# Placing a weight's sign on ScalarE, and squaring the first chunk's features on VectorE

## The chip, the cores and the metric

The kernel runs on one core of a Trainium2 chip. The core has a tensor engine (PE, with its weight loads PEld), a vector engine (DVE), a scalar engine (ACT), a general engine (POOL), and SP, whose queue issues transfers. Each engine works through its own list of instructions in order; they wait for each other by semaphores. The metric is device time in microseconds of one execution. The profile is of one execution, and its times are counted from the start of its span.

## What is computed

Attention of 8 batches, 8 heads, 576 positions and 64 dimensions, of which heads 0 to 3 see the last 32 positions and heads 4 to 7 every 32nd position. Its output goes as 4608 tokens of 512 features through an MLP with squared rectification:

```python
def _attn_ref(q, k, v):
    scores = scale * np.matmul(q, k.transpose(0, 1, 3, 2))
    mask_local = (rel >= 0) & (rel < stride)
    mask_strided = (rel >= 0) & (pos[None, :] % stride == pos[:, None] % stride)
    ...
    return np.matmul(attn, v).astype(np.float32)

def _moe_ref(x, w_in, w_out):
    h = np.maximum(x @ w_in, 0.0)
    return (h * h @ w_out).astype(np.float32)
```

`w_in` (512 x 2048) and `w_out` (2048 x 512) arrive as 64-bit floats. The kernel turns each into two 32-bit parts, a high and a low one, and each matrix product of the MLP is made of three: high x high, high x low, low x high.

## The kernel before

The tokens are cut into 12 chunks of 384. Chunk 0's attention comes first (`first` and `late`, 4 pairs of heads). Then a loop of steps `s` runs the MLP: step `s` belongs to chunk `c = s // 16` and to feature tile `j = s % 16` of 128 features. `up(c, j)` makes 12 matmuls into a PSUM tile `ph` (the trace's `h`), rectifies and squares it, copies it to `gh` and puts the remainder into `gl`; `down(c, j)` takes `gh` and `gl` with `w_out` in 9 matmuls into the outputs `y`. `down` runs two steps behind `up`. The attention of later chunks is laid between these steps: `local` and `strided` make chunk 1's while chunk 0's MLP runs.

The weights are converted by `convert` (lines 146 to 180) while attention and chunk 0's MLP run. There are 16 weight tiles `k` of 1024 columns, `w_in` and `w_out` in turn; tiles 0 to 11 come whole, tiles 12 to 15 in two halves each through the pool `s3` of five buffers, which the strided attention uses as well. A 64-bit float is two 32-bit words, `raw[:, :, 0]` and `raw[:, :, 1]`, the second with sign, exponent and upper mantissa. For each tile, `scale(k)` (line 152, ACT) takes that second word as a 32-bit float and multiplies it by 2^-112, which sets the exponent as a 32-bit float needs it three bits further up. Then, for each half of 512 columns, these run one after the other:

- `z` (line 164, ACT): the first word, scaled to its upper three bits, into a PSUM tile;
- the sign merge (line 167, DVE): the sign bit of the second word is put into `z`;
- the shift (line 168, DVE): the second word is shifted left by three, which throws its sign away, and `z` is merged in; this is the weight as a 32-bit float;
- `split`: the high part (line 171, ACT) and the low part (line 172, POOL). It is put on the lists one half later, behind the next half's `z`.

`zbank` names the PSUM banks that `z` may use: two at first, and one (bank 4) from step `s == LATER` (3) on, since the attention of chunk 1 needs the other. The conversion runs two halves a step in chunk 0 (`WRATE`). Its instructions are put behind `gh` of the step (`behind({"a": last["gh"]}, ...)`), and it is the list of ACT that this orders. Six halves are put ahead of the loop. The order of each engine's list is set when the kernel is built, by a planner that goes by its own estimates.

`p_t` are two tiles of 128 x 384 in SBUF, cleared at the start (line 114), of which the attention of chunks 2 and later (`pe_head`) writes parts, and in which it counts on zeros elsewhere. `p_t[1]` also serves as operand of the matmuls that keep PE busy at the start.

Of the kernel before, what the change touches and what calls it, by code (L numbers as in the profile page):

```python
# [11 lines left out]
AF = mybir.ActivationFunctionType  # L12
ALU = mybir.AluOpType
# [13 lines left out]
NFT = DF // P  # L27
# [22 lines left out]
def f32(ap):  # L50
    return ap.bitcast(F32)
# [35 lines left out]
def attn_moe(ctx: ExitStack, tc, qk_l, v_l, qk_d, v_d, qk_p, v_p, f_s, q_s, k_s, v_s, w_in, w_out, masks, eye, out):  # L87
    nc = tc.nc
# [13 lines left out]
    def psum(i, nm):  # L102

        return ps.tile([P, 512], F32, name=nm, tag=f"ps{i}")
# [4 lines left out]
    ident = const.tile([P, P], F32, name="ident")  # L109


    p_t = [const.tile([P, NW, QC], F32, name=f"p_t{i}") for i in range(2)]
    for t in p_t:
        nc.gpsimd.memset(t, 0.0)
# [16 lines left out]
    def fetch(k):  # L131

        p, which = order[k]
        src = (w_out if which else w_in)[p].bitcast(U32).rearrange("p (n t) -> p n t", t=2)
        if k < 12:
            raw = wpool.tile([P, 1024, 2], U32, name=f"raw{k}", tag=f"w{k + 8 if k < 8 else k + 4}")
            nc.sync.dma_start(out=raw, in_=src)
            raws[k] = [(raw, slice(0, 1024))]
        else:
            raws[k] = []  # L140
            for i in range(0, 1024, WP):
                raw = spool.tile([P, WP, 2], U32, name=f"raw{k}_{i}", tag="s3", bufs=5)
                nc.sync.dma_start(out=raw, in_=src[:, i : i + WP])
                raws[k].append((raw, slice(i, i + WP)))

    def convert():

        split = None

        def scale(k):  # L150
            for raw, _ in raws[k]:
                nc.scalar.mul(f32(raw[:, :, 1]), f32(raw[:, :, 1]), 2.0**-112)  # L152

        scale(0)
        for k in range(NFT):
            p, which = order[k]
            t = wpool.tile([P, 2, 1024], F32R, name=f"w{which}_{p}", tag=f"w{k}")
            (wo if which else wi)[p] = t[:, 0], t[:, 1]
            cuts = [(raw[:, i : i + WP], sl.start + i) for raw, sl in raws.pop(k) for i in range(0, sl.stop - sl.start, WP)]
            for raw, at in cuts:  # L160

                z = psum(zbank[next(zturn) % len(zbank)], f"z{k}_{at}").bitcast(U32)
                w, hi, lo = raw[:, :, 1], t[:, 0, at : at + WP], t[:, 1, at : at + WP]
                first_step = nc.scalar.activation(z, raw[:, :, 0], AF.Copy, bias=-0.49, scale=2.0**-29 * (1 - 2.0**-9))  # L164
                if split:
                    split()
                nc.vector.scalar_tensor_tensor(out=z, in0=w, scalar=0x80000000, in1=z, op0=ALU.bitwise_and, op1=ALU.bitwise_or)  # L167
                last["v"] = nc.vector.scalar_tensor_tensor(out=w, in0=w, scalar=3, in1=z, op0=ALU.logical_shift_left, op1=ALU.bitwise_or)  # L168

                def split(w=w, hi=hi, lo=lo, at=at, k=k):  # L170
                    last["a"] = nc.scalar.copy(hi, f32(w))  # L171
                    last["g"] = nc.gpsimd.tensor_sub(lo, f32(w), f32(hi))  # L172
                    if at and 4 <= k < 12:
                        fetch(k + 4)

                if not at and k + 1 < NFT and k + 1 in raws:
                    with tc.issue_after(first_step.ins):
                        scale(k + 1)
                yield
        split()  # L180
# [266 lines left out]
    def up(c, j):  # L447
        x = xt[c]
        p, o = divmod(j, 2)
        ph = psum((c * NFT + j) % 3, f"h{c}_{j}")  # L450
        n = 0
        for kt in range(4):
            kind, kk = "ls"[kt // 2], kt % 2
            xh, xl = x[kind, "h"][:, kk, :], x[kind, "l"][:, kk, :]
            wsl = slice(kt * 256 + o * P, kt * 256 + (o + 1) * P)
            for w, xx in ((wi[p][0], xh), (wi[p][0], xl), (wi[p][1], xh)):
                done = nc.tensor.matmul(ph[:, :TC], w[:, wsl], xx, start=n == 0, stop=n == 11)  # L457
                n += 1
        gh = gpool.tile([P, TC], F32R, name=f"gh{c}_{j}", tag="gh")
        gl = gpool.tile([P, TC], F32R, name=f"gl{c}_{j}", tag="gl")  # L460
        g = ph[:, :TC]
        nc.scalar.activation(g, g, AF.Relu)  # L462
        nc.scalar.activation(g, g, AF.Square)  # L463
        last["gh"] = nc.scalar.copy(gh, g)  # L464
        nc.vector.tensor_sub(gl, g, f32(gh))  # L465
        g_tiles[c, j] = gh, gl
        return done

    def down(c, j):
        gh, gl = g_tiles.pop((c, j))  # L470
        p, o = divmod(j, 2)
        if j == 0:
            y_ps[c] = [ps_y.tile([P, DM], F32, name=f"y{c}_{t}", tag="psy") for t in range(NTT)]
        wsl = slice(o * DM, (o + 1) * DM)
        for t in range(NTT):
            sl = slice(t * P, (t + 1) * P)
            for k, (g, w) in enumerate(((gh, wo[p][0]), (gh, wo[p][1]), (gl, wo[p][0]))):
                done = nc.tensor.matmul(y_ps[c][t], g[:, sl], w[:, wsl], start=j == 0 and k == 0, stop=j == NFT - 1 and k == 2)  # L478
        if j == NFT - 1:
            for t in range(NTT):  # L480
                y = ypool.tile([P, DM], F32, name=f"ysb{c}_{t}", tag="ysb")
                (nc.scalar.copy if t == 1 else nc.vector.tensor_copy)(y, y_ps[c][t])
                nc.sync.dma_start(out=out[c * TC + t * P : c * TC + (t + 1) * P, :], in_=y)
        return done


    def run(gen):
        for _ in gen:
            pass
# [37 lines left out]
    def local(c):  # L527
        heads = [pair_at(c, pr, True, pr, "3") for pr in range(2)]
        for h in (0, 0, 1, 0, 1, 0, 0, 1, 1, 1):
            next(heads[h])  # L530
            yield
# [15 lines left out]
    def take(c, which):  # L547

        if NPLAIN <= c < NCHUNK:
            for h in map(int, which):  # L550
                if (c, h) not in heads:
                    heads[c, h] = pe_head(c, h)
                with ExitStack() as st:
                    for i in (last["pe"], *(weights_end.values() if c == NPLAIN else ())):
                        st.enter_context(tc.issue_after(i.ins))
                    last.pop("mm", None)
                    next(heads[c, h])
                    last["pe"] = last.get("mm", last["pe"])
# [55 lines left out]
    for s in range(NS + 2):  # L614
        c, j = divmod(s, NFT)
        if s < NFT:
            up(c, j)
            if s >= 2:
                last["pe"] = down(*divmod(s - 2, NFT))

        elif s % 2 == 0:
            before, between, rest = plan[j // 2]
            for part, slots, two in (up, (s, s + 1), before), (down, (s - 2, s - 1), between):
                take(c + 1, two)
                with tc.issue_after(last["pe"].ins):
                    for i in slots:
                        if 0 <= i < NS:
                            last["mm"] = part(*divmod(i, NFT))
                last["pe"] = last["mm"]
            take(c + 1, rest)  # L630
        if j == NFT - 2:
            take(c + 2, "010")
        if c == 0:

            weights = behind({"a": last["gh"]}, ungated)
            for _ in range(WRATE):
                if next(weights, "end") != "end":
                    weights_end = {e: last[e] for e in "agsv"}
        if s == LATER:
            zbank = (4,)  # L640
        if c + 1 < NCHUNK and s >= LATER:
            j0 = LATER if c == 0 else 0
            if j == j0:
                lo, st = local(c + 1) if c == 0 else iter(()), strided(c + 1)
                if c == 0:
                    lo, st = behind(heads_end, lo), behind(heads_end, st)
                if c == 1:
                    st = behind(weights_end, st)
                cost = sum(2 * sum(range(i0 + 1, i1 + 1)) + 10 for _, i0, i1, _ in ranges(c + 1))
                dl = ds = 0  # L650
            fl, fs = ((j + 1 - j0) / n for n in SPREAD[min(c, 1)])
            while dl < fl * 10 and next(lo, "end") != "end":
                dl += 1
            while ds < fs * cost:
                k = next(st, "end")
                if k == "end":
                    break
                ds += k
            if j == NFT - 1:
                run(lo)  # L660
                run(st)
# [76 lines left out]
```

## Time and profile before

| | us |
|---|---|
| median of 3 runs | 892.15 (891.91 to 892.57) |
| the profiled execution | 893.0 |
| its span | 891.2 |
| DVE, lines 167 and 168, 32 each | 22.1 and 21.9 |
| ACT, lines 164 and 171, 32 each | 20.6 and 21.0 |
| ACT, line 152, 20 | 19.3 |
| POOL, line 172, 32 | 42.2 |

A row of the profile names the line, the engine, the operation, and `out<-in` by the program's names; then a count, the busy time, the mean of one in ns, and the idle time of the engine just before them with what ended it. `raw`, `z` and `w` belong to the conversion, `h`, `gh`, `gl` and `y` to the MLP; `pq`, `sc`, `pp`, `qkvs` to the strided attention, `e`, `nm`, `rs`, `pt`, `b` to the pairs of heads. In a row of stretches, engines follow in the order PE, PEld, DVE, ACT, POOL.

### The profile page before, as it was taken

What the parts mean: (1) busy time and instruction counts of PE and PEld (TensorE: products, weight loads), DVE (VectorE), ACT (ScalarE), POOL (GpSimd) and SP (SyncE); (2) the same over time, 40 slices, a digit from 0 to 9 for tenths busy, and PEclk for the clock granted to TensorE, in tenths of its full rate; (3) what the DMA queues carried; (4) which work ended last, traced back from release to release, by engine and by line L of the source; (5) the groups of instructions that cost most, each with busy time, mean ns of one, the idle gap of its engine ahead of it and who ended that gap; (6) DMA issues with size and microseconds to landing.
All of it is one profiled execution on the core that took longest, in us unless ns stands there. A gap on an engine that the chain in (4) does not pass through costs nothing.

```text
span 891.2 us, 14804 instructions
## 1 busy us (share of the span) xinstructions
PE 874.0 (98%) x4744; PEld 790.8 (89%) x4744; DVE 652.2 (73%) x1836; ACT 579.8 (65%) x1526; POOL 676.2 (76%) x720
## 2 busy tenths in 40 slices
PE   8898999999999999999999999999999999999997
PEld 7686789999999999899999999998999999998996
DVE  5689778878878878879678778787787887883111
ACT  5897986666757656757747657666665675664332
POOL 4679678788887889989888997997988899782000
PEclk9899999999999999999999999999999999999999
DMA  9833351323113114104202312211031121000000
GB/s 352 351 138 116 106 179 48 106 70 96 60 45 125 42 39 150 43 13 123 67 17 74 102 31 73 76 57 56 30 114 60 31 70 50 18 2 1 36 1 35
DMA packets 26797, 71.40 MB, mean 80 GB/s; under 512 B 2976, under 2 KB 8736, under 8 KB 25184
## 3 DMA queue, kind: packets, MB, share of 16 engines
q1 hardware_dynamic: 26432, 70.14, 23.8%
q8 instruction: 37, 0.61, 0.3%
q14 instruction: 40, 0.33, 0.1%
q10 hardware_dynamic: 288, 0.33, 0.1%
HBM read 61.01 MB, written 9.44 MB: 79 GB/s over the span
## 4 chain that ended last, share of the span: by engine, by line
PE 91%; ACT 4%; DVE 2%; POOL 2%; issue 1%; DVEq 0%; POOLq 0%; ACTq 0%
PE h L457 43%; PE y L478 42%; PE s L233 2%; PE o L279 2%; POOL w L172 1%; ACT e L340 1%; ACT raw L152 1%; DVE raw L168 1%; PE b L316 1%; DVE z L167 1%; PE w_ps L573 1%; ACT z L164 1%; ACT w L171 1%; PE b L373 0%; ACT pt L355 0%
## 5 line engine op out<-in xcount | busy, mean ns | idle before, releaser
L478 PE MATMUL y<-w,gh 128*128 128x512 f32 x1152 | 358.0, 392 | 4.3 <-ACT w L171 2.7
L478 PEld LDWEIGHTS y<-w,gh 128*128 128x128 f32 x1152 | 212.3, 188 | 46.2 <-ACT w L171 3.5
L457 PE MATMUL h<-xlh,w 128*128 128x384 f32 x768 | 229.4, 340 | 1.1 <-POOL w L172 0.6
L457 PE MATMUL h<-xsh,w 128*128 128x384 f32 x768 | 225.6, 335 | 0.8 <-POOL w L172 0.5
L478 PE MATMUL y<-w,gl 128*128 128x512 f32 x576 | 224.5, 392 | 0.7 <-DVE gl L465 0.7
L429 POOL TENSOR_TENSOR pp<-vs,sc 128x448 f32<-128x448 f32 (+10 forms) x192 | 189.7, 1012 | 40.3 <-DVE qs L430 18.1
L407 POOL TENSOR_TENSOR pq<-ks,qs 128x512 f32<-128x512 f32 (+2 forms) x192 | 197.8, 1049 | 18.8 <-DVE sc L408 14.4
L465 DVE TENSOR_TENSOR gl<-h,gh 128x384 fp32r<-128x384 f32 x192 | 105.4, 549 | 83.4 <-ACT gh L464 82.0
L462 ACT ACTIVATE h<-h 128x384 f32<-128x384 f32 x192 | 90.6, 473 | 109.5 <-PE h L457 106.5
L464 ACT CAST gh<-h 128x384 fp32r<-128x384 f32 x192 | 91.4, 477 | 105.6 <-PE y L478 104.6
L408 DVE TENSOR_REDUCE sc<-pq 128x8 f32<-128x512 f32 (+4 forms) x228 | 119.3, 534 | 43.9 <-POOL pq L407 41.8
L457 PEld LDWEIGHTS h<-xlh,w 128*128 128x128 f32 x768 | 141.8, 188 | 4.5 <-POOL w L172 1.3
L457 PEld LDWEIGHTS h<-xsh,w 128*128 128x128 f32 x768 | 141.2, 188 | 2.0 <-POOL w L172 0.9
L430 DVE TENSOR_REDUCE qs<-pp 128x64 f32<-128x448 f32 (+11 forms) x192 | 106.9, 563 | 32.0 <-POOL pp L429 30.4
L457 PE MATMUL h<-xll,w 128*128 128x384 f32 x384 | 129.3, 337 | 0.0
L478 PEld LDWEIGHTS y<-w,gl 128*128 128x128 f32 x576 | 108.0, 188 | 23.8 <-DVE gl L465 1.2
L457 PE MATMUL h<-xsl,w 128*128 128x384 f32 x384 | 128.2, 334 | 0.4 <-DVE xsl L378 0.4
L463 ACT ACTIVATE h<-h 128x384 f32<-128x384 f32 x192 | 90.5, 473 | 3.7
L258 DVE STREAM_TRANSPOSE p_t<-e 32x128 f32<-32x128 f32 x240 | 72.3, 301 | 10.3 <-ACT e L247 6.0
L457 PEld LDWEIGHTS h<-xll,w 128*128 128x128 f32 x384 | 72.5, 189 | 2.1
L457 PEld LDWEIGHTS h<-xsl,w 128*128 128x128 f32 x384 | 72.0, 188 | 0.6 <-DVE xsl L378 0.6
L242 ACT ACTIVATE e<-e,nm 96x128 f32<-96x128 f32 x160 | 62.5, 392 | 9.3 <-DVE nm L225 8.0
(85 smaller groups left out, 1088.5 us busy)
## 6 DMA issues: line engine op xcount, KB each, us to landing
qk<-qk_l SPq DMA_DIRECT2D x24, 400.0 KB, 3.2
y<-ysb SPq DMA_DIRECT2D x36, 256.0 KB, 3.2
raw<-w_in SPq DMA_DIRECT2D x7, 1024.0 KB, 10.8
qk<-qk_l SPq DMA_DIRECT2D x16, 416.0 KB, 3.2
vs<-v_s SPq DMA_DIRECT2D x10, 576.0 KB, 3.7
raw<-w_out SPq DMA_DIRECT2D x5, 1024.0 KB, 12.9
v<-v_l SPq DMA_DIRECT2D x40, 128.0 KB, 2.0
ks<-k_s SPq DMA_DIRECT2D x8, 576.0 KB, 3.8
```

Source lines behind the costliest of these rows:

```text
L242: nc.scalar.activation(e[:QC, cut(w)], e[:QC, cut(w)], AF.Exp, bias=nmax[:QC, w : w + 1], scale=-1.0, accum_out=ssum[:QC, w, :1])
L258: nc.vector.transpose(out=pt[STR * k : STR * (k + 1), :, STR * r : STR * (r + 1)], in_=e.rearrange("p (w k) -> p w k", k=KW)[STR * r : STR ...
L407: nc.gpsimd.tensor_mul(pv, kt[:, a : a + m, :], qt[:, i - i0 : i - i0 + 1, :].broadcast_to([P, m, D]))
L408: nc.vector.tensor_reduce(out=sc[:, i - i0, a : a + m], in_=pv, op=ALU.add, axis=AX.X)
L429: nc.gpsimd.tensor_mul(pv, vt[:, a : a + nd, :n], sc[:, il : il + 1, :n].broadcast_to([P, nd, n]))
L430: nc.vector.tensor_reduce(out=ot[:, il, a : a + nd], in_=pv, op=ALU.add, axis=AX.X)
L457: done = nc.tensor.matmul(ph[:, :TC], w[:, wsl], xx, start=n == 0, stop=n == 11)
L462: nc.scalar.activation(g, g, AF.Relu)
L463: nc.scalar.activation(g, g, AF.Square)
L464: last["gh"] = nc.scalar.copy(gh, g)
L465: nc.vector.tensor_sub(gl, g, f32(gh))
L478: done = nc.tensor.matmul(y_ps[c][t], g[:, sl], w[:, wsl], start=j == 0 and k == 0, stop=j == NFT - 1 and k == 2)
```

## The change

Two parts. In the conversion, the multiplication by 2^-112 becomes a rectification with a slope for negative values of -2^32. A negative word comes out positive and 2^32 times as large, which is one set bit in its exponent; the shift by three moves this bit to where the sign stands. A positive word comes out as before. So the sign merge is dropped.

In chunk 0, the square is no longer made by ACT. ACT writes the rectified features into `p_t` (turn about), and DVE multiplies the features, rectified once more, with them, into PSUM, from where `gh` and `gl` are made as before. Chunks 1 to 11 keep rectification and square on ACT. As `p_t` now gets other contents, it is cleared once more in step 15.

```diff
         def scale(k):
             for raw, _ in raws[k]:
-                nc.scalar.mul(f32(raw[:, :, 1]), f32(raw[:, :, 1]), 2.0**-112)
+                nc.scalar.activation(f32(raw[:, :, 1]), f32(raw[:, :, 1]), AF.Prelu, scale=2.0**-112, alpha=-(2.0**32))
...
                 if split:
                     split()
-                nc.vector.scalar_tensor_tensor(out=z, in0=w, scalar=0x80000000, in1=z, op0=ALU.bitwise_and, op1=ALU.bitwise_or)
                 last["v"] = nc.vector.scalar_tensor_tensor(out=w, in0=w, scalar=3, in1=z, op0=ALU.logical_shift_left, op1=ALU.bitwise_or)
...
         g = ph[:, :TC]
-        nc.scalar.activation(g, g, AF.Relu)
-        nc.scalar.activation(g, g, AF.Square)
+        if c == 0:
+            r = p_t[j % 2].rearrange("p w q -> p (w q)")
+            nc.scalar.activation(r, g, AF.Relu)
+            nc.vector.scalar_tensor_tensor(out=g, in0=g, scalar=0.0, in1=r, op0=ALU.max, op1=ALU.mult)
+        else:
+            nc.scalar.activation(g, g, AF.Relu)
+            nc.scalar.activation(g, g, AF.Square)
         last["gh"] = nc.scalar.copy(gh, g)
...
         if s == LATER:
             zbank = (4,)
+        if s == NFT - 1:
+            for t in p_t:
+                nc.gpsimd.memset(t, 0.0)
```

## The prediction

> **What bounds the kernel now.** I read first the page's span, then the busy time by stretch (columns: stretch, length, then busy time and count of PE, PEld, DVE, ACT, POOL, then PE's granted clock, the DMA share, GB/s), then the table of who waited for whom for PE between 38 and 115 us (total, times, longest).
>
> ```profile
> span 891.2 us, 14804 instructions
> 38.00:112.00 74.00, 66.58 (x359) 55.26 (x358) 61.31 (x123) 63.89 (x122) 57.98 (x62) 1.00 0.38 130
> 300.00:800.00 500.00, 500.00 (x2628) 457.45 (x2627) 399.48 (x1157) 327.80 (x907) 438.97 (x445) 1.00 0.19 59
> PE y L478 <- ACT w L171: 2.7, 2, 1.5
> PE y L478 <- ACT gh L464: 1.5, 1, 1.5
> PE h L457 <- POOL w L172: 1.1, 3, 0.5
> PE b L354 <- ACT pt L355: 0.7, 1, 0.7
> PE y L478 <- DVE gl L465: 0.7, 1, 0.7
> PE h L457 <- ACT w L171: 0.5, 1, 0.5
> PE y L478 <- POOL w L172: 0.2, 1, 0.2
> ```
>
> From 300 to 800 us PE is busy for all of 500 us. No faster vector or scalar work can shorten that part; what ends earlier ahead of it moves it forward as a block. What can be won lies where PE stands still: the first chunk, whose MLP runs while the weights are still being converted. Its waits from 38 to 115 us add up to 2.7 + 1.5 + 1.1 + 0.7 + 0.7 + 0.5 + 0.2 = 7.4 us, and the stretch row agrees: PE is busy 66.6 of 74. This is close to a ceiling. 4.5 us of it (the four rows with w) are waits for converted weights, 2.2 us the filling of the pipeline (gh and gl of the first step), 0.7 us an attention copy. In the same stretch DVE is busy for 61.3 of 74 us and ACT for 63.9: both are rather full, so work taken off either should be felt by the conversion, which runs on both.
>
> **The change part by part.** The durations of what goes, comes and is altered (last fields: busy us, mean ns, then idle before):
>
> ```profile
> L167 DVE SCALAR_TENSOR_TENSOR z<-raw,z 128x512 uint32<-128x512 uint32 x32 | 22.1, 690 | 10.6 <-ACT z L164 10.5
> L168 DVE SCALAR_TENSOR_TENSOR raw<-raw,z 128x512 uint32<-128x512 uint32 x32 | 21.9, 683 | 0.9
> L164 ACT ACTIVATE z<-raw 128x512 uint32<-128x512 uint32 x32 | 20.6, 644 | 4.8 <-DVE raw L168 4.7
> L152 ACT ACTIVATE raw<-raw 128x1024 f32<-128x1024 f32 (+1 forms) x20 | 19.3, 974 | 1.5 <-POOL w L172 1.0 <-DMA raw<-w_out 0.5
> L462 ACT ACTIVATE h<-h 128x384 f32<-128x384 f32 x192 | 90.6, 473 | 109.5 <-PE h L457 106.5 <-DVE sc L408 1.1 <-DVE qs L430 1.1
> L463 ACT ACTIVATE h<-h 128x384 f32<-128x384 f32 x192 | 90.5, 473 | 3.7
> L464 ACT CAST gh<-h 128x384 fp32r<-128x384 f32 x192 | 91.4, 477 | 105.6 <-PE y L478 104.6
> L321 DVE SCALAR_TENSOR_TENSOR e<-b,mask_sb 96x384 f32<-96x384 f32 x4 | 2.1, 526 | 0.0
> L465 DVE TENSOR_TENSOR gl<-h,gh 128x384 fp32r<-128x384 f32 x192 | 105.4, 549 | 83.4 <-ACT gh L464 82.0 <-PE y L478 0.2
> L114 POOL MEMSET p_t<- 128x384 f32 x2 | 0.8, 417 | 0.3 <-POOLq L726 0.3
> ```
>
> *Removed on DVE:* the sign merge, line 167, 32 times 0.690 us = 22.1 us.
>
> *Added on DVE:* 16 products (max with 0, times the rectified copy) of 128x384, one operand and the result in PSUM. Not in this trace; the nearest rows are line 321 at 0.526 and line 465 at 0.549 us, the dearest 0.690 (line 167, a longer row of 512). I take 0.55: 16 x 0.55 = 8.8 us. DVE's net is -13.3 us (bounds 22.1 - 8.4 = 13.7 and 22.1 - 11.0 = 11.1).
>
> *Removed on ACT:* 16 squares (line 463) of 0.473 = 7.6 us. The 16 rectifications stay; their result now goes to SBUF in place of PSUM, which line 464 (gh, from PSUM to SBUF) does at 0.477 against 0.473: nothing.
>
> *Altered on ACT:* the 20 scalings (line 152) become a sloped rectification. Three different functions of one size cost 0.473, 0.473 and 0.477 us in lines 462 to 464, so I put the difference at 0; the 4 ns spread over 20 gives 0.1 us as the upper bound, unless a table must be loaded (a rival below).
>
> *Added on POOL:* two memsets of 0.417 us at step 15. They wait for the last two products, and the multiplications of chunk 1's stage queue behind them on POOL. POOL is busy 439 of 500 us afterwards while PE never waits, so 0.8 us plus a stall of a step hides in that slack; the cleared tiles are first used by the attention of chunk 2, a whole chunk ahead of its use. 0 on the path. No DMA is added or moved.
>
> *The path.* Conversion of one half tile runs z (ACT, line 164), sign merge (DVE, 167), shift and merge (DVE, 168), high part (ACT, 171), low part (POOL, 172). From step 3 on z has one PSUM bank only, so the next z can't start before line 168 of the half before has read it: a loop of 0.644 + 0.690 + 0.683 = 2.0 us a half, 4.0 us for the two of a step, without any other work in between, and then DVE's queue comes on top. The order in time shows both (start, length, instruction, idle before):
>
> ```profile
> 82.47 0.68 DVE L167 SCALAR_TENSOR_TENSOR z<-raw,z 128x512 uint32<-128x512 uint32 x1
> 83.23 0.67 DVE L168 SCALAR_TENSOR_TENSOR raw<-raw,z 128x512 uint32<-128x512 uint32 x1
> 83.94 0.64 ACT L164 ACTIVATE z<-raw 128x512 uint32<-128x512 uint32 x1 [1.55 <-DVE raw L168]
> 85.35 0.68 DVE L167 SCALAR_TENSOR_TENSOR z<-raw,z 128x512 uint32<-128x512 uint32 x1
> 86.06 0.69 DVE L168 SCALAR_TENSOR_TENSOR raw<-raw,z 128x512 uint32<-128x512 uint32 x1
> 86.79 0.63 ACT L164 ACTIVATE z<-raw 128x512 uint32<-128x512 uint32 x1 [0.58 <-DVE raw L168]
> 87.36 0.63 ACT L171 CAST w<-raw 128x512 fp32r<-128x512 f32 x1
> 88.05 0.96 PE L478 MATMUL y<-w,gh 128*128 128x512 f32 x3 [1.21 <-ACT w L171]
> 78.82 0.97 PE L478 MATMUL y<-w,gh 128*128 128x512 f32 x3 [1.50 <-ACT w L171]
> ```
>
> ACT stands 1.55 us for DVE, then 0.58 us again, and at the end of this chain PE stands 1.21 us. Without line 167 the loop is 1.33 us a half.
>
> *What of the 4.5 us goes.* If each wait lost only the one 0.69 us of its own half, the two long ones (1.50 and 1.21) would keep 0.8 + 0.5 and the short ones (all under 0.69) vanish: 3.2 us won. But the delay adds up over the halves of the loop (the wait at 88.05 has two merges of 0.68 us in the rows above), so up to 4.5 can go. I take 3.9. For the attention copy (0.7 us) I take 0.3: squares no longer stand in ACT's queue ahead of it, but its own producer stays. For the filling (2.2 us) I take 0: the chain from PE to gh goes from 0.473 + 0.473 + 0.477 on one engine to 0.473 + 0.55 + 0.477 over two, 0.08 us longer and two hand-overs more, while the merges ahead of it on DVE are gone; bounds -0.8 and +0.8.
>
> *The new wait.* gh on ACT now waits for DVE. Behind it on ACT stand z, the high parts and the scalings of the next halves, and for these PE waits. Bounds: 0, where other work of ACT lies between (as it lies between many rectifications and squares now), and 16 x 0.55 = 8.8 us of ACT, which would eat the 7.6 us won. I take it at 0 in the sum, since DVE sheds more than it gets, and keep the upper end as a rival.
>
> *Before 38 us* the same merge goes from the first halves. Attention there sets the end; bounds from the clock, which was granted at half speed in parts of it (the next to last field of the first row is 0.50). A group of 32 small products took twice as long there as another of the same shape later:
>
> ```profile
> 26.00:28.00 2.00, 2.00 (x26) 1.77 (x22) 0.55 (x1) 0.47 (x1) 1.48 (x2) 0.50 1.02 426
> 24.98 3.14 PE b L373 x32
> 31.48 1.59 PE L373 MATMUL b<-pt,v 96*32 96x96 f32 x32
> ```
>
> A shift of the short gaps can win or lose one such difference, 3.14 - 1.59 = 1.5 us. I take 0.
>
> *Sum:* 3.9 + 0.3 + 0 + 0 + 0 = 4.2 us. The profiled execution took 893.0 us (span 891.2 and 1.8 around it), so 888.8; the median of the three runs, 892.15, lies 0.85 below it: 888.0 us.
>
> **Rivals.**
>
> *A. The table.* A slope needs a function that this kernel has not used. The trace has one table load for all of ACT's functions, and exponentials lie among the scalings:
>
> ```profile
> L565 ACT ACT_TABLE_LOAD x1 | 1.3, 1283 | 1.2 <-PEq L726 1.2
> L343 ACT ACTIVATE e<-e 96x384 f32<-96x384 f32 (+1 forms) x8 | 4.6, 570 | 0.0
> ```
>
> If the sloped function isn't in the table that holds the exponential, ACT must load twice around each of these 8 exponentials that has scalings on both sides: up to 8 x 2 x 1.283 = 20.5 us, less 7.6 us of squares, 13 us more on an engine that has 74 - 64 = 10 us free in the stretch. 3 to 13 us go onto the path, 8 in the middle: about 900, slower. It decides from 6 loads on (6 x 1.283 = 7.7, ACT's whole relief). For it: nothing in the trace shows this function. Against: rectification, square, copy and exponential all ran after a single load. [...] 6%.
>
> *B. ACT waits for DVE.* The 16 new waits cost their upper bound, 8.8 us: ACT is 1.2 us worse off, DVE still better. Then the conversion keeps about half of its waits (2 us won) and the filling loses up to 0.8 at each of two steps: 891 to 894, no change. For it: DVE works in order, and a subtraction of 36 elements in its queue once took 1.95 us. Against: the net relief of 13 us on that engine.
>
> ```profile
> 79.80 1.95 DVE L414 TENSOR_TENSOR sc<-sc,mx 128x36 f32<-128x36 f32 x1
> ```
>
> 15%.
>
> *C. The last weights come too late.* Four half tiles are fetched only when a strided tile gives its buffer free:
>
> ```profile
> SPq L143 <- POOL xsl L441: 25.7, 1, 25.7
> 99.11 0.33 SPq L143 DMA_DIRECT2D raw<-w_out  x1
> raw<-w_out SPq DMA_DIRECT2D x4, 512.0 KB, 4.0
> 110.03 1.32 POOL L172 TENSOR_TENSOR w<-raw,w 128x512 fp32r<-128x512 f32 x1 [0.88 <-ACT w L171]
> ```
>
> The first of them is converted at 110.03 + 1.32 = 111.35. If the strided work doesn't move, the least chain from 99.11 is 4.0 us of transfer (the median of these issues) and at most 0.97 + 0.64 + 0.68 + 0.63 + 1.32 = 4.2 us of work: 107.3, so the 4 us of the forecast are just allowed; with the queues in between, only 2 may be: 890. 12%.
>
> *D. More than forecast:* all 7.4 us, or 4.2 and the 1.5 us of the clock: 884.7 to 886. 7%.
>
> **How the numbers follow.** The forecast, 886 to 890, has 60%. D lies faster, C is at the edge of it; about 0.2% (1.8 us) is what a measurement can tell from no change, so faster means under 890.4. Forecast and D give 67, half of C 6: 0.73. Same: 11 of B's 15 and the rest of C, 0.17. Slower: A, and the end of B (4), 0.10. The range from 884.7 (D) to 893.0 (most of B) leaves out A and B's end.
>
> **What would show it.** Right: DVE's shift-and-merge follows z at once; ACT's waits for it (4.7 us in 6) fall under 2 us; PE's waits for w fall from 4.5 to about 0.6 us; the steady stretch of the second chunk starts some 4 us earlier and looks the same. Wrong: more than one table load (A); rows "ACT gh <- DVE h" of several us (B); waits of the scaling for DMA, and PE's waits gathered after 100 us (C); a span before 38 us that differs by over 1 us (clock).

## The result, and the profile after

The changed kernel takes 886.95 us (median of 5 runs, 885.92 to 889.13) where the one before takes 892.15 (891.43 to 892.57): a ratio of 0.9941, with a 95% interval of 0.9926 to 0.9957, or 5.2 us less. The forecast was 888.0, 4.2 less. Run again later it came to 886.97 against 892.96 (0.9931, 0.9914 to 0.9948), 6.0 less. So the direction and the place were right, and the gain was put some 1 to 2 us too low.

The page's span line and the two stretches of the prediction, after (columns as before):

```profile
span 885.2 us, 14792 instructions
38.00:112.00 74.00, 72.02 (x395) 63.54 (x394) 56.86 (x119) 62.99 (x118) 63.74 (x72) 0.98 0.43 148
300.00:800.00 500.00, 500.00 (x2628) 457.26 (x2627) 400.03 (x1151) 326.59 (x900) 438.00 (x444) 1.00 0.19 58
```

The steady part is what it was: PE busy for 500 of 500 us, with the same number of matmuls. In the first chunk PE is now busy for 72.0 of 74 us instead of 66.6, and DVE for 56.9 instead of 61.3. That is the stretch of the forecast. Who PE waited for in the first 115 us (total, times, longest):

```profile
PE y L485 <- ACT gh L471: 2.0, 1, 2.0
PE h L458 <- DVE raw L169: 1.8, 1, 1.8
PE w_ps L580 <- POOL sums L120: 1.6, 1, 1.6
PE b L363 <- ACT pt L356: 1.5, 3, 0.7
PE b L374 <- ACT pt L356: 1.3, 1, 1.3
PE b L355 <- POOL e L349: 0.9, 2, 0.4
```

No row names `w`: the 4.5 us of waits for converted weights are gone to the last one. Between 38 and 115 us the first row is the only one left, 2.0 us of 7.4. The others lie before 38 us, the second of them new: a matmul of `up` that takes the PSUM bank of a `z` (below). The groups of the conversion and of the first chunk's MLP (busy us, mean ns, idle before):

```profile
L169 DVE SCALAR_TENSOR_TENSOR raw<-raw,z 128x512 uint32<-128x512 uint32 x32 | 21.9, 684 | 9.0 <-ACT z L166 8.7
L467 DVE SCALAR_TENSOR_TENSOR h<-h,p_t 128x384 f32<-128x384 f32 x16 | 9.0, 560 | 4.2 <-ACT p_t L466 4.1
L166 ACT ACTIVATE z<-raw 128x512 uint32<-128x512 uint32 x32 | 20.6, 644 | 0.0
L154 ACT ACTIVATE raw<-raw 128x1024 f32<-128x1024 f32 x12 | 14.0, 1168 | 0.0
L466 ACT ACTIVATE p_t<-h 128x384 f32<-128x384 f32 x16 | 7.9, 499 | 6.2 <-PE h L458 6.2
L471 ACT CAST gh<-h 128x384 fp32r<-128x384 f32 x20 | 9.7, 490 | 2.0 <-DVE h L467 1.6 <-PE y L485 0.4
L572 ACT ACT_TABLE_LOAD x1 | 1.3, 1283 | 1.2 <-PEq L736 1.2
```

Read the last fields. `z` waited 4.7 us for the shift and now waits for nothing. Among these rows ACT's longest idle time is now one for PE (6.2 us ahead of line 466) and no longer one for DVE. The table is still loaded once.

### The profile page after: what moved, and what is told of

Read it like the earlier page. It is cut to its first block, busy times and chain, and to the rows that moved or that the text cites. A ratio compares the mean times of both kernels' runs of the same rounds, so it can differ in the third digit from the quotient of the medians.

```text
span 885.2 us, 14792 instructions
## 1 busy us (share of the span) xinstructions
PE 871.1 (98%) x4744; PEld 792.5 (90%) x4744; DVE 640.3 (72%) x1820; ACT 572.1 (65%) x1510; POOL 677.3 (77%) x722
## 4 chain that ended last, share of the span: by engine, by line
PE 96%; DMA 2%; ACT 1%; POOL 1%; DVE 0%; issue 0%; DVEq 0%; POOLq 0%; ACTq 0%
PE h L458 45%; PE y L485 45%; PE s L234 2%; PE o L280 2%; DMA qk<-qk_d 2%; ACT e L341 1%; PE w_ps L580 1%; PE b L317 1%; PE b L363 0%; POOL pq L408 0%; POOL w L173 0%; PE b L355 0%; DVE e L322 0%; ACT raw L154 0%; DVEq L739 0%
## 5 line engine op out<-in xcount | busy, mean ns | idle before, releaser
L469 ACT ACTIVATE h<-h 128x384 f32<-128x384 f32 x176 | 82.9, 471 | 109.7 <-PE h L458 109.2
L470 ACT ACTIVATE h<-h 128x384 f32<-128x384 f32 x176 | 83.3, 473 | 3.6
```

## The experiments

Each was timed in five rounds against the kernel before, on one chip within a group. Edits are to the changed kernel if nothing else is said. The expectations weigh these theories: **L**, the loop on the single PSUM bank carried the gain; **D**, it was DVE's load as such, wherever in the loop or out of it the work stands; **A** (not the rival A of the prediction), the 7.6 us of squares that ACT sheds were needed as well; **F**, what is left lies in the filling of the pipeline at the start; **K**, the pause of PE there lowers its clock behind it; **T**, DVE's load costs only from a threshold on.

| kernel | us (lowest to highest) | ratio to before (95%) |
|---|---|---|
| E1, sign part alone | 888.85 (887.95 to 889.04) | 0.9955 (0.9943 to 0.9967) |
| E2, square part alone | 896.73 (893.99 to 896.94) | 1.0038 (1.0026 to 1.0050) |
| E3, a bit operation a half, off the loop | 902.81 (902.04 to 903.35) | 1.0112 (1.0099 to 1.0125) |
| E6, a reduction a half, off the loop | 893.92 (893.50 to 895.09) | 1.0010 (1.0001 to 1.0018) |
| E11, the same for every other half | 887.30 (885.79 to 890.19) | 0.9947 (0.9934 to 0.9960) |
| E7, kernel before with two `z` banks | 908.40 (904.84 to 909.66) | 1.0166 (1.0145 to 1.0186) |
| E5, first two tiles squared on ACT | 887.40 (885.15 to 889.35) | 0.9941 (0.9927 to 0.9955) |
| E8, PE kept busy ahead of the first `down` | 887.00 (886.89 to 889.42) | 0.9938 (0.9924 to 0.9952) |
| E9, `up` kept in order | 886.56 (885.81 to 888.07) | 0.9931 (0.9918 to 0.9944) |
| E10, E9 and E5 | 887.14 (886.76 to 887.36) | 0.9939 (0.9927 to 0.9951) |
| E12, E9 without the square part | 887.85 (886.59 to 889.05) | 0.9948 (0.9936 to 0.9960) |
| the changed kernel again | 886.97 (885.62 to 889.82) | 0.9931 (0.9914 to 0.9948) |

### Each part alone: E1 and E2

E1 keeps the sloped rectification and leaves squares on ACT:

```diff
-        if c == 0:
+        if False:
...
-        if s == NFT - 1:
-            for t in p_t:
-                nc.gpsimd.memset(t, 0.0)
```

> The sign part alone: the merge is gone, squares stay on ACT in chunk 0, no second clearing. Theory L (the loop z, merge, shift over one PSUM bank held the conversion): PE's waits for w fall from 4.5 us to under 1.5, time 886.5 to 889. Rival A (ACT's 7.6 us of squares were as needed): with ACT at its old load the waits for w stay over 2.5 us, 889.5 to 892.

E2 keeps the products and puts the old sign back:

```diff
-                nc.scalar.activation(f32(raw[:, :, 1]), f32(raw[:, :, 1]), AF.Prelu, scale=2.0**-112, alpha=-(2.0**32))
+                nc.scalar.mul(f32(raw[:, :, 1]), f32(raw[:, :, 1]), 2.0**-112)
...
+                nc.vector.scalar_tensor_tensor(out=z, in0=w, scalar=0x80000000, in1=z, op0=ALU.bitwise_and, op1=ALU.bitwise_or)
```

> The square part alone: products on DVE in chunk 0, the merge stays. Theory L: the loop is as long as before and DVE has 8.8 us more to do, PE's waits for w stay at 4 us or more, 891 to 895. Rival A: ACT's relief wins 2 to 3 us, 888.5 to 890.5.

E1 wins 3.9 us (892.78 to 888.85) and E2 loses 3.4 to 4.0 (by the ratio, by the medians). Together they win 5.2 to 6.0. The parts do not add up, and the profiles say in part why. PE's waits in E1 between 38 and 112 us:

```profile
PE b L355 <- DVE xll L379: 1.5, 1, 1.5
PE y L485 <- ACT gh L471: 1.5, 1, 1.5
PE y L485 <- DVE gl L472: 1.4, 1, 1.4
PE h L458 <- DVE gl L472: 0.4, 1, 0.4
```

The waits for `w` are gone with the merge alone; what is left is for the most part the filling at the start (`gh` and the first `gl`, 2.9 us) and an attention copy. DVE is then busy for 48.4 of 74 us, and ACT is the full engine, 19.7 of 20 us in the second of these stretches of E1 (order PE, PEld, DVE, ACT, POOL):

```profile
38.00:112.00 74.00, 69.23 (x382) 59.55 (x382) 48.43 (x102) 68.47 (x134) 62.56 (x68) 1.00 0.43 148
80.00:100.00 20.00, 18.09 (x108) 15.58 (x107) 12.90 (x30) 19.73 (x40) 18.72 (x19) 1.00 0.16 52
```

There a shift of work from ACT to DVE can be worth something. In E2 the merge still fills DVE, and the same shift brings no relief. E2's stretch, and whom its ACT waits for from 38 to 112 us:

```profile
38.00:112.00 74.00, 66.67 (x351) 56.01 (x350) 63.53 (x135) 57.01 (x106) 57.24 (x61) 0.95 0.34 120
```

```profile
ACT z L166 <- DVE raw L170: 5.3, 5, 2.2
ACT p_t L467 <- PE h L459: 3.5, 4, 2.5
ACT gh L472 <- DVE h L468: 2.3, 1, 2.3
```

ACT was relieved (57.0 us busy instead of 63.9), yet it stands 5.3 us for the shift (4.7 before) and 2.3 us for the product. This is the mechanism of the prediction's rival B. PE's waits for `w` stay: from 38 to 125 us they add up to 4.0 us (4.5 before). The largest row of them, and a stretch of 2 us a little later:

```profile
PE y L486 <- ACT w L173: 2.0, 2, 1.7
82.00:84.00 2.00, 2.00 (x7) 1.61 (x6) 1.65 (x4) 2.00 (x5) 1.24 (x1) 0.50 0.00 0
```

That the square part alone gains nothing is shown. Its loss, which lies above both expectations, is mostly something else in this profile. From 38 us to the first group of 24 products of the steady part (118.51 us in E2, 115.34 before) PE stands still for 8.0 us instead of 7.4, but is busy for 72.5 instead of 69.9, at a granted clock of 0.96 instead of 1.00. The half clock lies at about 79 to 86 us (granted 0.97 from 60 to 80 us, 0.86 from 80 to 100, and 1.00 in each stretch of 2 us from 86 to 100), behind a wait for `w` of 1.7 us. The kernel before has waits of 1.5 and 1.2 us there and keeps its clock at 1.00, so whether the square part brings the half clock about is open.

So the square part alone is no gain, and beside the sign part it is likely one. How large a gain is less sure: 888.85 - 886.95 = 1.9 us here and 1.3 us between E12 and E9, with intervals that overlap both times.

### Loop or load: E3, E6, E11 and E7

The merge was two things at once: a third step in the loop of z, merge and shift, and 22.1 us of DVE time. E3 and E6 put the time back behind the shift, where `z`'s bank is already free. E3, with a bit operation on the low word that nobody reads again:

```diff
                 last["v"] = nc.vector.scalar_tensor_tensor(out=w, in0=w, scalar=3, in1=z, op0=ALU.logical_shift_left, op1=ALU.bitwise_or)
+                lw = raw[:, :, 0]
+                nc.vector.scalar_tensor_tensor(out=lw, in0=lw, scalar=0x80000000, in1=lw, op0=ALU.bitwise_and, op1=ALU.bitwise_or)
```

> The changed kernel with one more DVE operation a half (a bit operation that leaves the low word as it is), as long as the merge was, but behind the shift, off the loop of z. Theory L (length of the loop): 886 to 889, PE's waits for w under 1.5 us. Rival D (DVE's total load, 22 us, was what held): the gain goes again, 890 to 893, waits for w of 3 us or more.

It measured something else. E3's groups:

```profile
L171 DVE SCALAR_TENSOR_TENSOR raw<-raw 128x512 uint32<-128x512 uint32 x32 | 34.4, 1075 | 0.0
L175 POOL TENSOR_TENSOR w<-raw,w 128x512 fp32r<-128x512 f32 x32 | 48.8, 1528 | 18.7 <-ACT w L174 17.7 <-DVE sc L423 0.7 <-DVE gl L474 0.3
```

The operation took 1.075 us in the mean, not 0.69, and POOL's low part went up to 1.528 us each. E3 says nothing on loop against load, and something on DVE and POOL running at the same time (last section). E6 uses an operation with one input instead, a maximum over the half into an unused column:

```diff
                 last["v"] = nc.vector.scalar_tensor_tensor(out=w, in0=w, scalar=3, in1=z, op0=ALU.logical_shift_left, op1=ALU.bitwise_or)
+                nc.vector.tensor_reduce(out=mask_sb[:, 3, P - 1 :], in_=f32(w), op=ALU.max, axis=AX.X)
```

> The changed kernel with one more DVE operation a half behind the shift, off the loop of z: a maximum over the half (one operand, about 0.67 us as line 322's), 21 us in all, so that DVE's load is what it would be with the merge. The square part alone, which has this load inside the loop, took 896.7. Theory L (length of the loop): 886 to 890, PE's waits for w under 1.5 us. Rival D (DVE's load): 893 to 897, waits for w of 3 us or more.

E6's reduction had the size wanted, and left POOL alone:

```profile
L170 DVE TENSOR_REDUCE mask_sb<-raw 128x1 f32<-128x512 f32 x32 | 21.7, 678 | 0.3
L174 POOL TENSOR_TENSOR w<-raw,w 128x512 fp32r<-128x512 f32 x32 | 42.0, 1317 | 19.9 <-ACT w L173 19.9
```

Off the loop, the merge's time costs 893.92 - 886.97 = 7.0 us: the whole gain and a little more. E6's waits of PE from 38 to 112 us, and a stretch:

```profile
PE y L486 <- ACT gh L472: 2.8, 1, 2.8
PE h L459 <- DVE gl L473: 1.4, 1, 1.4
PE y L486 <- ACT w L173: 1.0, 1, 1.0
PE y L486 <- POOL w L174: 0.9, 1, 0.9
PE h L459 <- POOL w L174: 0.4, 1, 0.4
```

```profile
80.00:100.00 20.00, 16.16 (x92) 13.06 (x91) 19.62 (x41) 15.67 (x30) 15.91 (x17) 1.00 0.07 23
```

DVE is busy 19.6 of 20 us, PE 16.2, and the waits for `w` are back at 2.3 us; the row of `gl` lies in this stretch too (at 95.9 us), that of `gh` in the filling at the start. What the place in the loop adds at this load is at most the step from E6 to E2, which has nearly the same DVE work with the merge in the loop: 896.73 - 893.92 = 2.8 us. The waits for `w` grow by 1.7 us of it (2.3 to 4.0); the clock differs too, 0.98 in E6 and 0.95 in E2 from 38 to 112 us. At this load D is the larger part and L the smaller one. E11 puts in the reduction for one half in two:

```diff
+                if at == 0:
+                    nc.vector.tensor_reduce(out=mask_sb[:, 3, P - 1 :], in_=f32(w), op=ALU.max, axis=AX.X)
```

> Half of the load that cost 7 us: the maximum off the loop for every other half only, 16 of them, 10.9 us on DVE. Theory D (DVE's load in chunk 0 sets it, once it is nearly full): 889 to 891.5, DVE busy for some 61 of 74 us from 38 to 112. Rival T (a threshold: the merge's load mattered only where it made DVE full): within 1 us of the changed kernel, 886 to 888.

887.30: half the load, some 10.9 us of DVE, costs 0.3 us, and the second half of it 6.6. E11 ran on another chip than E6; by the ratios the first half costs 1.4 us (0.9947 against 0.9931), with intervals that overlap, so it can't be told from nothing; run by run, at the same granted clock, the times coincide (last section). The cost isn't in proportion to the load, as T says: DVE's time is nearly free up to a point, and of the second half some six tenths are paid for (6.6 of 10.9). Where the point lies isn't shown by two loads.

Where the kernel before stands to this point matters for the verdict on L. By the sums, E11's DVE does 22.1 - 9.0 - 10.9 = 2.2 us less than that kernel's, and E6's 8.6 more. E11 is 5 us faster than it with nearly the same DVE work, and has no wait for `w` left. Its stretch, and the longer of its two waits of PE from 38 to 112 us (the other is one of 0.3 for `gl`):

```profile
38.00:112.00 74.00, 70.46 (x379) 61.49 (x377) 60.27 (x128) 62.12 (x116) 60.94 (x66) 0.95 0.41 140
PE y L487 <- ACT gh L473: 3.3, 1, 3.3
```

DVE is busy 60.3 of 74 us here and 61.3 in the kernel before, with its 4.5 us of waits for `w`. So relief of DVE alone isn't all of the gain: E11 differs from that kernel also by the squares taken off ACT and by the merge out of the loop. This speaks for L at that load, but doesn't show it, as E11 with the squares on ACT was not run. E7 tried the loop from the other side, with the kernel before and a second bank for `z` throughout:

```diff
-        if s == LATER:
-            zbank = (4,)
```

> The kernel before, merge and squares as they were, but z keeps two PSUM banks in turn all along (it shares one with chunk 1's local attention). Theory L: ACT's waits of z for the shift fall from 4.7 us to under 2, PE's waits for w from 4.5 to about 2, 888.5 to 890.5. Rival D: DVE is as full as before, no gain, 891.5 to 893.5; the same where the shared bank makes attention and conversion wait for each other.

15 us slower. The bank that `z` keeps is one that the attention needs. PE's three largest waits in E7 from 38 us on:

```profile
PE y L478 <- ACT w L171: 3.9, 2, 3.1
PE h L457 <- ACT w L171: 3.9, 1, 3.9
PE b L354 <- DVE raw L168: 2.6, 1, 2.6
```

ACT's wait for the shift did vanish, but transposes (`b`) now wait 2.6 us for a shift to give the bank free, and the waits for `w` are longer than before. The granted clock falls too (0.95 from 38 to 112 us, 1.00 before). It isn't a clean test of the loop, and no other was run at the load of the kernel before. How that kernel's 4.5 us divide between the loop, the squares on ACT and the last of DVE's load stays open.

### The start: E5, E8, E9, E10 and E12

What is left to win lies ahead of 44 us. The order in time around the first `gh`, after (start, length, instruction, idle before):

```profile
40.98 0.49 DVE L409 TENSOR_REDUCE sc<-pq 128x5 f32<-128x320 f32 x1 [0.41 <-POOL pq L408]
41.38 0.56 DVE L467 SCALAR_TENSOR_TENSOR h<-h,p_t 128x384 f32<-128x384 f32 x1
...
41.98 0.48 ACT L471 CAST gh<-h 128x384 fp32r<-128x384 f32 x1 [1.58 <-DVE h L467]
```

The first product queues behind reductions of the strided attention, which themselves wait for POOL, and ACT stands 1.58 us for it. E5 leaves the first two tiles to ACT:

```diff
-        if c == 0:
+        if c == 0 and j >= 2:
```

> The changed kernel with the squares of features 0 and 1 of chunk 0 on ACT. Theory F (the first product stands behind the strided sums on DVE, and the wait for it, 2.0 us, is the price of the change at the filling): the first down projection starts about 1 us earlier, 885 to 886.5. Rival: it isn't the product but the rest of the filling, within 0.5 us of the changed kernel, 886.5 to 887.5.

The wait for `gh` fell to 1.4 us with 0.4 for `gl`, 1.8 in place of 2.0, and the time is the same. E8 fills PE's gap there with 20 small products that nobody reads, to see whether the clock then holds:

```diff
-            up(c, j)
+            u_ins = up(c, j)
+            if s == 2:
+                with tc.issue_after(u_ins.ins):
+                    w_ps = ps_y.tile([P, 512], F32, name="w_ps_b", tag="psy")
+                    for _ in range(20):
+                        nc.tensor.matmul(w_ps[:, :P], zt, zt, start=True, stop=True)
```

> The changed kernel with 20 small matmuls, whose result nobody reads, ahead of the first down projection, in the 2 us in which PE waits for gh. Theory K (that pause drops PE's clock to half for the 3 us behind it): the clock stays at 1.0 from 42 to 48 us, about 1.3 us less, 885 to 886.3. Rival: the clock falls for the earlier pause at 32 us or not at all, 886.5 to 887.5; a little longer if the matmuls run past gh.

They ran too early to cover the gap; PE still waited 2.1 us for `gh`, the clock was granted at 0.50 in one stretch of 2 us behind it (44 to 46 us), and the time didn't change. Inconclusive. E9 takes up the 1.8 us wait for the bank of a `z`: the planner had put the products of `up` of the first tiles into each other on PE, and E9 keeps them in order. E10 is E9 with E5's condition.

```diff
-            up(c, j)
+            with ExitStack() as ups:
+                if s in (1, 2):
+                    ups.enter_context(tc.issue_after(last["up"].ins))
+                last["up"] = up(c, j)
```

> The changed kernel with the up projections of features 0, 1 and 2 held in order on PE's list (the planner had put them into each other, so that all three end together at 40.5 us and gh of the first waits behind them). Theory F (what is left is this filling): gh and gl of feature 0 are made while features 1 and 2 run, PE's wait for gh falls from 2.0 us to under 0.5, 884.5 to 886. Rival: PE waits as long at the start of feature 0 for the attention's result, 886.5 to 887.5.

> The same as the run with the up projections in order, and squares of features 0 and 1 on ACT. If the first product still stands behind the strided sums on DVE and PE waits for it: 0.3 to 1 us less than that run. If the order alone hides it: the same within 0.5 us.

The waits for the bank and for `gh` disappear, and one of 2.87 us for tokens takes their place (order in time of PE in E9):

```profile
34.36 0.44 PE L458 MATMUL h<-xsh,w 128*128 128x384 f32 x1 [2.87 <-ACT xsh L378]
```

0.4 us less than the changed kernel, within its spread; E10 0.2 more. This points to the attention's own chain as what sets the pace at the start; no order of MLP work tried here wins against it. E12 is E9 without the square part, as in E1:

> The sign part alone, with the up projections in order: what the square part is worth on top of the sign part, away from the filling. Rival A' (ACT's 7.6 us are needed as well): 1.5 to 2.5 us over the run in order with both parts. Rival: the square part only shifts the filling, within 0.7 us of it.

887.85, between E9 and E1, and 1.3 us over E9, which lies between the two expectations. None of these versions beats the changed kernel clearly.

## The prediction, step by step

**What bounds the kernel** was right: PE after the first chunk, the conversion in it. The steady block moved forward unchanged. The chain of work in order of time (start, length) has its first group of 24 products of `up`, before and after, at:

```profile
115.34 4.19 PE h L457 x24
```

```profile
109.15 4.19 PE h L458 x24
```

It starts 6.2 us earlier and is as long as it was.

**The part costs** held. The product took 0.560 us for an assumed 0.55. The scaling took 1168 ns as a sloped rectification, the same as its form of the same size before:

```profile
L152 ACT ACTIVATE raw<-raw 128x1024 f32<-128x1024 f32 x12 | 14.0, 1168 | 0.0
```

The one price wrongly put at nothing is the rectification into SBUF: 0.499 against 0.473 us, 16 x 0.026 = 0.4 us of ACT, hidden.

**"What of the 4.5 us goes. I take 3.9"** is the mis-sized term: all 4.5 went. So is the attention copy: 0.3 taken, its row of 0.7 in that stretch gone. The filling was taken at 0; its waits fell from 2.2 to 2.0 us. That makes 4.5 + 0.7 + 0.2 = 5.4 us less waiting from 38 to 115 us. It was dealt out per wait ("each wait lost only the one 0.69 us" at worst), as if a full engine gave back only what was taken from the one chain in view. E1 shows what took its place: with DVE at 48 of 74 us, no wait for `w` was left at all, whichever chain it hung on.

**"The path"** led to the right waits by a reason that is only partly borne out. The working followed the loop of 2.0 us a half and named the queue on DVE only as what "comes on top". In the runs the queue is no trifle: the merge's time, put back outside the loop, costs 7.0 us beside the products, and the place in the loop at most 2.8 more. But half of that time costs next to nothing, and E11 has no wait for `w` with DVE nearly as busy as before. This fits the loop as what held the kernel before, but its share there wasn't separated from that of the squares on ACT. The sentence in the part on what bounds the kernel, that DVE and ACT are "both rather full, so work taken off either should be felt by the conversion", held for DVE (E1) and failed for ACT where DVE stayed full (E2: waits for `w` of 4.0 us, against 4.5).

**"The new wait" at 0** was right. It shows as one wait of 1.6 us of ACT for a product, at the start (the row `ACT gh` above), against an upper bound of 8.8.

**"Before 38 us"**, taken at 0, left out two terms of opposite sign. (Its reading of the clock's field is off: in a row of stretches the granted clock is the last but two, so 0.50 in the first row is right, but not "next to last".) The new wait of 1.8 us for a `z`'s bank is one term. The other is the clock, granted at 0.71 from 24 to 26 us and 0.50 from 26 to 28 before, and at 1.00 and 0.66 after: the group of 32 small products that took 3.14 us before took 1.99 in the profile after:

```profile
25.00 1.99 PE L374 MATMUL b<-pt,v 96*32 96x96 f32 x32 [1.34 <-ACT pt L356]
```

That 1.15 us can't be put down to the change: E1, E2, E10, E11 and E12 show 3.14 or 3.15 us for it again, each with 0.50 granted from 26 to 28 us. So the 6.2 us by which the steady part starts earlier go as follows. PE stands still for 3.3 us less: 5.4 less from 38 us on, and 2.1 more before it, 1.8 of them for the bank. The other 2.9 are PE time that the profile counts as busy, and 1.15 of them are this group. For the 1.7 that are left, one reason would fit: a product lasts 0.33 us but the next starts 0.17 after it (before, order in time):

```profile
35.50 0.33 PE L457 MATMUL h<-xlh,w 128*128 128x384 f32 x1
35.67 0.33 PE L457 MATMUL h<-xsh,w 128*128 128x384 f32 x1
```

so that a stop costs its idle time and some 0.16 us of a product that runs out alone. Nine stops fewer from 38 to 115 us (ten before, one after) would be 1.4 us. This is an estimate and was not tested, and the clock works against it: it was granted at 0.50 from 44 to 46 us in this profile of the changed kernel and at 1.00 in that of the kernel before. How these 1.7 us divide stays open.

**The rivals.** A (table): one load, 1.283 us, as before, so what a second would cost wasn't measured. B (ACT waits for DVE): here only the one wait of 1.6 us; in E2, where the merge stays, ACT's waits of this kind are longer, though they are not most of E2's loss. C (the last weights late) failed because the strided work ahead of them moved too: the first of the four fetches started at 92.85 us in place of 99.11, in one group of SP's queue:

```profile
92.85 6.28 SPq L144 DMA_DIRECT2D raw<-w_out  x4
```

Its allowance of 4 us took the release of the buffer as fixed. D (884.7 to 886) and the forecast (888.0) have the median between them: the waits for `w` and the copy went as in D, the filling as in the forecast. D's second way, 4.2 us and 1.5 of the clock, comes to 892.15 - 5.7 = 886.5 and not 886, so it lay inside the forecast's range.

## What to carry to other kernels

Ask which engines have no slack in the stretch that counts: the first 10.9 us of added DVE work were nearly free here, and of the next 10.9 six tenths came onto the path. The move of work from ACT to DVE brought nothing alone, where DVE had been busy for 61.3 of 74 us, and is a likely gain beside the other part, where DVE was busy for 48.4; so try each part of a pair alone. When a variant is slower, look at the granted clock as well as at the waits. A loop seen in the order of time is a hypothesis: put its time back at another place of the same engine, and see whether the cost returns.

## What the runs showed of the hardware

**DVE and POOL at the same time.** The bit operation of E3 with both inputs and its output in SBUF took 1.075 us in the mean (0.67 at 72.39 us, 4.18 at 90.05), and POOL's subtraction rose from 1.317 (E6) to 1.528. Two of them (E3, order in time):

```profile
90.05 4.18 DVE L171 SCALAR_TENSOR_TENSOR raw<-raw 128x512 uint32<-128x512 uint32 x1
93.65 1.77 POOL L175 TENSOR_TENSOR w<-raw,w 128x512 fp32r<-128x512 f32 x1
```

The first ends 0.6 us after the second has begun, which takes 1.77 us, where the five rows of its kind in E6 between 98 and 110 us take 1.31 to 1.34. The shift of E3, the same kind of operation on DVE with one input in PSUM, took 0.677, and E6's reduction with one input in SBUF 0.678. Of these three only the one with both inputs in SBUF took longer, and POOL's subtraction was longer beside it. Why, no run here shows.

**The clock between executions of one program.** The two profiles of the changed kernel differ by 885.2 - 883.8 = 1.4 us of span with the same instructions. Stretches of 2 us in the first and in the second profile:

```profile
44.00:46.00 2.00, 2.00 (x7) 1.61 (x6) 1.83 (x4) 2.00 (x5) 0.97 (x1) 0.50 0.00 0
```

```profile
44.00:46.00 2.00, 2.00 (x12) 1.89 (x11) 1.85 (x3) 2.00 (x5) 0.76 (x1) 1.00 0.00 0
```

After a wait for `gh` of 2.0 us in the first and 1.8 in the second, PE's clock was granted at 0.50 and at 1.00. The steady block starts at 109.15 and at 107.81, 1.3 us apart. So nearly the same gap was followed by two different clocks in two executions of one program. What decides between them, no run here shows.

The runs show more of it. The ten runs of the changed kernel follow the mean granted clock: 885.6 to 885.9 us at 0.996 and 0.998, 886.95 to 886.98 at 0.992 and 0.993, 889.1 and 889.8 at 0.988 and 0.987. The 17 runs of the kernel before that were timed beside the last five don't: 891.6 and 892.6 at 0.998, 892.5 and 892.9 at 0.988. So the gain was some 6 us at the higher clock and some 3 at the lower one. E11's runs lie on the changed kernel's: 885.79 at 0.998, 887.28 and 887.31 at 0.993, 889.4 and 890.19 at 0.987. On a gain of 5 us this spread is most of it, and one run of each kernel would not have sized it.
